# A fused attention and dense block on one core: how the feature weights are loaded and spread, and the order of the first steps

## The chip, the core and the metric

The kernel runs on one core of a Trainium2 chip, as one launch. The core has five engines with a queue each: TensorE (PE; its weight loads are listed apart, as PEld), VectorE (DVE), ScalarE (ACT), GpSimd (POOL) and SyncE (SP), which here issues most of the transfers. An engine works through its queue in order; a step that needs another engine's result waits on a semaphore, and all that is queued behind it on its own engine waits with it. The metric is the device time of one execution in microseconds, the median of several runs.

## The reference, cut to what matters

```python
xn = _layernorm(x)                                   # x: 2048 tokens x 512
qkv = xn @ wqkv                                      # 32 heads of 16
pq = einsum("bhsd,hdf->bhsf", q, w_phi)              # w_phi: 32 x 16 x 16
pk = einsum("bhsd,hdf->bhsf", k, w_phi)
phi_q = concatenate([softmax(pq), softmax(-pq)])     # over 16 features
phi_k = concatenate([softmax(pk), softmax(-pk)])
kv = einsum("bhsf,bhsd->bhfd", phi_k, v);  z = phi_k summed over tokens
o = einsum("bhqf,bhfd->bhqd", phi_q, kv) / (einsum("bhqf,bhf->bhq", phi_q, z) + 1e-6)
h = xn @ w1 + b1                                     # 1792 hidden
return x + o @ wo + (h * tanh(softplus(h))) @ w2     # Mish
```

All inputs are bf16. Since k is used only through `w_phi`, the kernel multiplies the keys' weights and `w_phi` into one matrix first: the logits of the keys' features are `xn @ (wk @ blockdiag(w_phi))`. It does the same for the queries later.

## The kernel before

The 2048 tokens are 16 tiles of 128, in four groups of four. The whole program is one list of short steps, `STEPS` (L24 to L59), each with a name and numbers; a table (`run`, L627) maps the name to a function. The order in the list is the order in which each engine gets its work, since the schedule is made by hand (`tc.manual_schedule()`, L129); nothing reorders it afterwards. `@n` is the PSUM bank of a product, and a last letter `a`, `v` or `p` the engine of a copy or an operation (ScalarE, VectorE, GpSimd). What stands ahead of the list in the code, L475 to L520, is queued first.

The steps of the head, as far as the change touches them:

- The loads ahead of the list: token tiles 0 and 1 (L478), the first half of the keys' weights as they lie (`wkp[:, 0:2]`, L482), the other half through a transposing transfer into `wT` (L483), tiles 2 and 3 (L489), the values' weights `wv` (L490), half of `w1` (L491), tokens 4 to 7 (L492), the other half of `w1` (L493), all from SyncE; the bias `b1` and `w_phi` from ScalarE (L486, L488). `w_phi` comes in its final layout `wsrc`: 128 partitions, with four pieces of 16 elements in each.
- The constants: `ident` for turning with TensorE, `block` (ones where a row and a column belong to the same head), both made on GpSimd, and warm-ups: 12 products of ones that nobody reads (L519), nine of 512 columns and three of 128, in bank 5.
- `LS i`, `RS i`, `AZ i`: a tile's statistics (VectorE), its inverse root (ScalarE with Ln and Exp, or GpSimd) and its centring (VectorE). `TP i` turns the tile by four products with `ident`, `TC i` copies it into `xnT`.
- `TW kt` turns a quarter of the keys' weights from `wkp`, `TK kt` copies it into `wT`. `KM` makes the masks. `WB` (L527) multiplies `block` with `wsrc` into `Wbd`, the block diagonal of `w_phi` in four pieces. `F0 kt` folds: four products of `wT` with `Wbd`; `FD kt` copies the folded quarter back into `wkp`.
- `LP` (L197): the key logits of tiles 0 and 1, eight products of 512 columns, alternating between the tiles. `L s i` are the logits of the other tiles, `LC` their copy, `V t` and `VC t` the values and their copy, `H u` and `M u` the hidden layer's product and its Mish (with the bias `b1f`, made by `PB`, `CB`). `E`, `X`, `S` are the features (differences to the extremes, exponentials, sums). `AM` loads ScalarE's table for Mish. `LN g` and `AP g k` are statistics and centring of a later group, turned by transposing transfers. `DX`, `DW` load later tokens and weights.

TensorE's queue before: warm-ups, `PB`, `TW 0`, `TW 1`, `TP 0`, `TP 1`, `F0 0` to `F0 3`, `LP`, `V 1`, `TP 2`, `V 0`, `TP 3`, `L 0 2`, `H 0`, `L 0 3`, `H 1` and so on.

Of the kernel before, what the change touches and what calls it, by code (L numbers as in the profile page):

```python
# [8 lines left out]
BF16 = mybir.dt.bfloat16  # L9
# [3 lines left out]
ALU = mybir.AluOpType  # L13
# [17 lines left out]
DW 2; E 0 1; X 0 1; LN 2; LC 1 0 v; LC 1 3 v; WL 1; LN 3; AP 2 0; AP 2 1; X 0 0; V 6 @3; M 10; M 11;  # L31
M 12; H 14 @5; S 0 0; WL 2; LC 1 2 a; VC 6 a; M 13; AP 3 0; H 15 @0; H 16 @2; H 17 @1; LC 1 1 a; AP
3 1; WT; H 18 @3; H 19 @4; M 14; M 15; M 16; M 17; H 20 @5; M 18; M 19; H 21 @0; H 22 @2; H 23 @1; H
24 @3; M 20; M 21; H 25 @4; H 26 @5; M 22; M 23; H 27 @0; M 24; M 25; M 26; M 27; H 28 @2; M 28; H
29 @1; M 29; E 1 0; E 1 1; S 0 1; L 2 1 @3; L 2 0 @4; LC 2 0 v; L 2 2 @5; LC 2 1 v; L 2 3 @0; F 0
@2; R 0 0 a; L 3 2 @1; R 0 1 a; LC 2 2 v; LC 2 3 a; FC 0 a; X 1 0; F 1 @4; F 2 @3; FC 2 a; N 0 0; L
3 0 @5; V 9 @0; LC 3 0 a; V 3 @2; VC 3 a; LC 3 2 v; A 0 0; VC 9 a; V 7 @1; F 3 @3; V 2 @5; VC 7 a; V
8 @2; L 3 3 @0; FC 3 a; X 1 1; VC 2 a; FC 1 v; E 2 0; L 4 0 @4; DW 3; LC 3 3 a; E 2 1; V 4 @1; N 0
1; VC 8 v; X 2 0; S 1 1; LC 4 0 a; S 1 0; L 4 3 @3; VC 4 a; L 4 2 @5; V 11 @0; A 0 1; LC 4 2 a; V 5
@2; VC 11 a; R 1 1 a; S 2 0; L 4 1 @4; LC 4 1 a; L 3 1 @1; VC 5 a; LC 3 1 a; H 30 @5; H 31 @0; LC 4  # L40
3 v; R 1 0 a; M 30; H 32 @4; M 31; M 32; H 33 @2; M 33; N 1 1; H 34 @1; H 35 @3; H 36 @5; M 34; H 37
@0; M 35; H 38 @4; E 3 0; H 39 @2; H 40 @1; M 36; N 1 0; M 37; M 38; M 39; H 41 @3; H 42 @5; H 43
@0; M 40; A 1 0; M 41; E 3 1; M 42; M 43; A 1 1; X 2 1; V 12 @4; VC 12 a; L 5 0 @2; V 10 @1; V 15
# [19 lines left out]
def kernel(  # L63
# [12 lines left out]
    nc = tc.nc  # L76
    P = 128
# [15 lines left out]
    wphi_v = A_w_phi.rearrange("(j i) a b -> (i a) j b", j=4)  # L93
# [18 lines left out]
    wsrc = wts.tile([P, 4, DH], BF16, name="wsrc")  # L112
    wv = wts.tile([P, KT, D], BF16, name="wv")
# [8 lines left out]
    ident = consts.tile([P, P], BF16, name="ident")  # L122
    mhalf = consts.tile([P, TPG], FP32, name="mhalf")
# [9 lines left out]
    tables = ["natural_log_exp_and_others"]  # L133
# [343 lines left out]
    for t in range(2):  # L477
        nc.sync.dma_start(x_sb[:, t, :], x_v[:, t, :])  # L478


    wT_of = {0: lnp.tile([P, 4, 512], BF16, name="wT", tag="xn")}
    nc.sync.dma_start(wkp[:, 0:2, :], wqkv_v[:, 0:2, D : 2 * D])  # L482
    nc.sync.dma_start_transpose(  # L483
        out=wT_of[0][:, :, 2 * P : 4 * P], in_=A_wqkv[2 * P : 4 * P, D : 2 * D]
    )
# [3 lines left out]
    nc.sync.dma_start(x_sb[:, 2:4, :], x_v[:, 2:4, :])  # L489
    nc.sync.dma_start(wv[:], wqkv_v[:, :, 2 * D : 3 * D])  # L490
    nc.sync.dma_start(w1_sb[:, :, 0 : 7 * P], w1_v[:, :, 0 : 7 * P])  # L491
    nc.sync.dma_start(x_sb[:, 4:8, :], x_v[:, 4:8, :])  # L492
    nc.sync.dma_start(w1_sb[:, :, 7 * P : F], w1_v[:, :, 7 * P : F])  # L493

    nc.scalar.preload_act_table_set(tables[0])
    make_identity(nc, ident[:])

    nc.gpsimd.memset(block[:], 1.0)
# [6 lines left out]
    nc.gpsimd.memset(mhalf[:], -0.5)  # L505
    nc.gpsimd.memset(eps[:], 1e-5)
# [12 lines left out]
    for n in (512,) * WARM + (P,) * SHORT:  # L519
        dummy(n)  # L520

# [5 lines left out]
    def weights_by_block():  # L527
        nc.vector.tensor_tensor(
            out=Wbd[:].rearrange("p j (h e) -> p j h e", h=8),
            in0=block[:, None, :, :].to_broadcast([P, 4, 8, 16]),  # L530
            in1=wsrc[:, :, None, :].to_broadcast([P, 4, 8, 16]),
            op=ALU.mult,
        )
# [89 lines left out]
    def load_queries():  # L623
# [4 lines left out]
        "KM": masks, "AW": lambda: dummy(P), "WB": weights_by_block, "PB": bias,  # L628
        "AM": lambda: table("mish"), "CB": lambda: nc.vector.tensor_copy(b1f[:], pf_of.pop("b")[:, 0:FT]),
        "LS": first_stats, "RS": first_root, "AZ": first_apply, "TP": first_turn,  # L630
        "TW": turn_keys, "TK": lambda kt, c: keep_keys(kt, copies[c]),
# [49 lines left out]
```

## Time and profile before

| | us |
|---|---|
| runs before | 173.4, 173.81, 174.56 |
| median | 173.81 |
| span of the profiled execution (first to last instruction) | 172.0 |
| TensorE busy within it | 168.0 |
| VectorE, ScalarE busy | 143.9, 123.8 |
| GpSimd busy | 7.8 |

The profile's own execution is told by its span; what lies between that and the device time (start and end of the program) is not in the trace. Times in the views are microseconds from the span's start. In a row of the timeline stand start, duration, engine, line, operation, what it writes and reads, and how often; in brackets the idle time of the engine before it and what ended that. The chain of waits follows the work back from the last instruction: at each step to what released it, or to the instruction before it on its engine. A transfer's time runs from its issue to its landing.

### The profile page before, as it was taken

What the parts mean: (1) busy time and instruction counts of PE and PEld (TensorE: products, weight loads), DVE (VectorE), ACT (ScalarE), POOL (GpSimd) and SP (SyncE); (2) the same over time, 40 slices, a digit from 0 to 9 for tenths busy, and PEclk for the clock granted to TensorE, in tenths of its full rate; (3) what the DMA queues carried; (4) which work ended last, traced back from release to release, by engine and by line L of the source; (5) the groups of instructions that cost most, each with busy time, mean ns of one, the idle gap of its engine ahead of it and who ended that gap; (6) DMA issues with size and microseconds to landing.
All of it is one profiled execution on the core that took longest, in us unless ns stands there. A gap on an engine that the chain in (4) does not pass through costs nothing.

```text
span 172.0 us, 2735 instructions
## 1 busy us (share of the span) xinstructions
PE 168.0 (98%) x1047; PEld 82.6 (48%) x1047; DVE 143.9 (84%) x223; ACT 123.8 (72%) x199; POOL 7.8 (5%) x23
## 2 busy tenths in 40 slices
PE   8899999999999999999999999999999999999993
PEld 2554444444454544454445644544444444554452
DVE  3869998999599999969989999799799998884333
ACT  2778899997999989889978989977282792432200
POOL 4123002300000000000000000000000000000000
PEclk9999999999999999999999999999999999999999
DMA  4997299589000000000000194309335618668941
GB/s 124 303 370 248 54 255 347 99 162 228 21 0 0 0 4 0 0 0 0 4 0 0 36 113 99 61 9 150 90 97 116 153 52 197 146 134 216 110 131 61
DMA packets 44185, 18.02 MB, mean 105 GB/s; under 512 B 35980, under 2 KB 44172, under 8 KB 44172
## 3 DMA queue, kind: packets, MB, share of 16 engines
q1 hardware_dynamic: 43472, 17.73, 43.9%
q8 instruction: 8, 0.13, 0.4%
q10 hardware_dynamic: 700, 0.12, 0.4%
q14 instruction: 5, 0.04, 0.1%
HBM read 7.10 MB, written 2.10 MB: 53 GB/s over the span
## 4 chain that ended last, share of the span: by engine, by line
PE 95%; DMA 2%; SPq 0%; ACT 0%; issue 0%; DVE 0%
PE po L457 28%; PE ph L223 28%; PE pl L189 14%; PE po L464 8%; PE pv L189 8%; PE pnd L412 2%; PE pkv L381 2%; DMA wkp<-in_A_wqkv_dram 2%; PE pl L204 1%; PE pfold L151 1%; PE pwide L189 1%; SPq L478 0%; PE ptr L569 0%; PE ptw L576 0%; ACT wT L582 0%
## 5 line engine op out<-in xcount | busy, mean ns | idle before, releaser
L457 PE MATMUL po<-w_sb,acts 128*128 128x512 bf16 (+2 forms) x238 | 50.8, 366 | 0.0
L223 PE MATMUL ph<-xnT,w_sb 128*128 128x512 bf16 x224 | 49.8, 379 | 0.0
L234 ACT ACTIVATE acts<-ph,b1f 128x512 bf16<-128x512 f32 x56 | 36.3, 701 | 4.2 <-PE ph L223 4.0
L300 DVE TENSOR_REDUCE s<-e 128x128 f32<-128x2048 bf16 x16 | 36.1, 2276 | 0.5 <-ACT e L283 0.5
L223 PEld LDWEIGHTS <-w_sb 128*128 128x128 bf16 x224 | 21.7, 98 | 25.7
L457 PEld LDWEIGHTS <-acts 128*128 128x128 bf16 x238 | 22.1, 98 | 23.6
L283 ACT ACTIVATE e<-e 128x2048 bf16<-128x2048 bf16 x16 | 30.5, 1919 | 0.0
L189 PEld LDWEIGHTS <-xnT 128*128 128x128 bf16 x184 | 17.5, 98 | 19.6
L471 DVE TENSOR_TENSOR x_sb<-po,x_sb 128x512 bf16<-128x512 f32 (+2 forms) x17 | 11.0, 656 | 8.4 <-PE po L464 8.4
L464 PE MATMUL po<-wqk,xnT 128*128 128x512 bf16 (+2 forms) x68 | 15.6, 366 | 0.0
L189 PE MATMUL pv<-wv,xnT 128*128 128x512 bf16 x64 | 15.6, 379 | 0.0
L189 PE MATMUL pl<-wqk,xnT 128*128 128x512 bf16 x64 | 15.4, 379 | 0.0
L427 ACT COPY ds<-pnd 128x32 f32<-128x32 f32 x16 | 2.9, 182 | 16.5 <-PE pnd L412 16.5
L247 ACT CAST p_sb<-pl 128x512 bf16<-128x512 f32 x21 | 12.2, 594 | 3.6 <-PE pl L189 3.4
L139 ACT ACT_TABLE_LOAD x10 | 12.8, 1283 | 0.2
L258 DVE TENSOR_TENSOR m<-m 128x512 bf16<-128x512 bf16 (+1 forms) x32 | 11.5, 359 | 1.1
L189 PE MATMUL pl<-wkp,xnT 128*128 128x512 bf16 x48 | 11.7, 379 | 0.0
L267 DVE TENSOR_TENSOR e<-p_sb,m 128x2048 bf16<-128x2048 bf16 x8 | 9.8, 1226 | 1.8 <-PE pkv L381 1.5
L258 DVE TENSOR_TENSOR m<-p_sb 128x1024 bf16<-128x1024 bf16 x16 | 10.9, 681 | 0.0
L165 DVE BATCH_NORM_STATS2 stats<-x_sb 128x6 f32<-128x512 bf16 x16 | 10.1, 677 | 0.9 <-DMA x_sb<-in_A_x_dram 0.9
L267 DVE TENSOR_TENSOR e<-m,p_sb 128x2048 bf16<-128x2048 bf16 x8 | 9.8, 1225 | 0.3
L334 DVE TENSOR_TENSOR e<-e,r 128x2048 bf16<-128x2048 bf16 x8 | 9.6, 1216 | 0.5 <-ACT r L309 0.5
(68 smaller groups left out, 133.9 us busy)
## 6 DMA issues: line engine op xcount, KB each, us to landing
w_sb<-in_B_w_dram SPq DMA_DIRECT2D x4, 896.0 KB, 7.8
out_dram<-x_sb SPq DMA_DIRECT2D x15, 128.0 KB, 1.8
x_sb<-in_A_x_dram SPq DMA_DIRECT2D x3, 512.0 KB, 7.5
wv<-in_A_wqkv_dram SPq DMA_DIRECT2D x1, 512.0 KB, 4.6
wqk<-in_A_wo_dram SPq DMA_DIRECT2D x1, 512.0 KB, 4.9
x_sb<-in_A_x_dram SPq DMA_DIRECT2D x2, 128.0 KB, 2.1
wkp<-in_A_wqkv_dram SPq DMA_DIRECT2D x1, 256.0 KB, 3.6
x_sb<-in_A_x_dram SPq DMA_DIRECT2D x1, 256.0 KB, 3.6
```

The costliest lines, as they stand in the source:

```text
L139: nc.scalar.preload_act_table_set(name)
L189: nc.tensor.matmul(pp, lhsT=xnT[:, t, kt, :], rhs=w[:, kt, :], start=(kt == 0), stop=(kt == KT - 1),)
L223: nc.tensor.matmul(ph_of[u][:], lhsT=w1_sb[:, kt, f * P : (f + 1) * P], rhs=xnT[:, g * TPG : (g + 1) * TPG, kt, :], start=(kt == 0), stop= ...
L234: nc.scalar.activation(acts[:, f, g * 512 : (g + 1) * 512], ph_of.pop(u)[:], ACT.Mish, bias=b1f[:, f : f + 1])
L247: copy(p_of[s][:, i, :], pl_of.pop((s, i)))
L258: nc.vector.tensor_tensor(out=m[:], in0=src[:, :, 0:half], in1=src[:, :, half : 2 * half], op=op)
L267: nc.vector.tensor_tensor(out=e_of[s][:].rearrange("p t j l c -> p (t j) l c")[:, :, pl, :].rearrange("p t (c e o) -> p t c e o", e=8, o=2 ...
L283: nc.scalar.activation(v, v, ACT.Exp)
L300: nc.vector.reduce_sum(t[:], pair(s, k).rearrange("p t j l (c e) -> p (t j l c) e", e=16), axis=AX.X)
L457: nc.tensor.matmul(po_of[t, c.stop][:, c], lhsT=acts[:, f, t * P : (t + 1) * P], rhs=w2_sb[:, f, c], start=(f == 0), stop=False,)
L464: nc.tensor.matmul(po_of[t, c.stop][:, c], lhsT=oT_of[t // 2][:, t % 2 * 4 + j, :], rhs=wo_sb[:, j, c], start=False, stop=(j == 3),)
L471: nc.vector.tensor_tensor(out=y, in0=po_of.pop((t, c.stop))[:, c], in1=y, op=ALU.add)
```

## The change

Five things change together.

1. `w_phi` is loaded by rows into a new tile `wraw` (128 partitions with one piece of 64 elements each), and a new step `WX` spreads it into the layout of `wsrc` by 16 small products with a selection matrix `sel`; `WC` copies the result from PSUM. `sel` lies in the space of `kvm`, which is used much later.
2. The warm-ups become steps: `AW 512` or `AW 128`. They stand before, around and behind `WX`: in all seven of 512 and two of 128 columns.
3. The loads become steps (`D`), and the half of the keys' weights goes ahead of token tile 1.
4. `WB` can run on GpSimd (`WB p`), and does. The clearing of constants goes from GpSimd to VectorE, and ScalarE's first table is loaded by the first step that needs it.
5. The steps of the head are in another order and partly on other engines, up to the hidden products of the first group. From `H 13` on the list is as it was.

```diff
-WARM, SHORT = 9, 3
 STEPS = """
-KM; LS 0; RS 0 p; LS 1; RS 1 a; DX 2; PB @0; AZ 0; AZ 1; TW 0 @1; TW 1 @2; TP 0 @3; TP 1 @4; TK 0 a;
-TK 1 a; WB; F0 0 @5; FD 0 a; F0 1 @1; TC 0 v; F0 2 @2; F0 3 @3; FD 2 a; TC 1 v; FD 1 v; FD 3 a; LP i
-@4,5; LS 2; LS 3; RS 2 a; LC 0 0 a; V 1 @1; RS 3 p; AZ 2; TP 2 @2; TC 2 a; VC 1 a; AM; V 0 @3; LC 0
-1 v; AZ 3; CB; TP 3 @4; TC 3 v; L 0 2 @5; LC 0 2 a; H 0 @0; M 0; L 0 3 @2; LC 0 3 a; H 1 @1; M 1; H
-2 @4; M 2; H 3 @5; H 4 @0; H 5 @2; VC 0 a; H 6 @1; M 3; M 4; M 5; H 7 @4; M 6; M 7; H 8 @3; H 9 @5;
-H 10 @0; M 8; H 11 @2; H 12 @1; LN 1; M 9; E 0 0; AP 1 0; AP 1 1; H 13 @4; L 1 0 @3; DX 3; L 1 3 @5;
+D x001 s; AW 512; AW 512; AW 512; AW 512; AW 512; AW 128; D phi a; D wn02 s; D b1 a; D x011 s; AW
+512; WX @3; AW 512; LS 0; D wt1 s; WC v; WB p; AW 128; TW 1 @5; KM; RS 0 a; TW 0 @3; TK 1 a; LS 1;
+F0 1 @2; TK 0 v; F0 0 @0; AZ 0; TP 0 @1; D x022 s; RS 1 a; FD 1 a; FD 0 a; AZ 1; PB @4; TC 0 v; TP 1
+@5; F0 2 @2; F0 3 @3; FD 2 a; TC 1 v; LS 2; D wv s; CB; RS 2 p; LS 3; FD 3 a; AZ 2; D w10007 s; LP i
+@0,1; RS 3 p; V 0 @2; AZ 3; TP 2 @5; V 1 @3; LC 0 0 a; TC 2 a; D x044 s; LC 0 1 v; TP 3 @5; TC 3 a;
+TL; L 0 2 @0; H 4 @5; M 4; D w10714 s; VC 0 v; L 0 3 @2; VC 1 v; DX 2; LC 0 2 v; H 6 @1; H 1 @5; LN
+1; H 2 @3; H 3 @0; LC 0 3 a; H 0 @2; M 2; M 6; M 1; H 5 @3; E 0 0; AM; M 3; H 9 @1; M 0; H 7 @4; M
+9; AP 1 0; H 8 @5; H 12 @1; H 11 @2; M 7; H 10 @0; AP 1 1; H 13 @4; M 5; L 1 0 @3; DX 3; M 8; L 1 3
...
-    wphi_v = A_w_phi.rearrange("(j i) a b -> (i a) j b", j=4)
+    wraw = wts.tile([P, 4 * DH], BF16, name="wraw")
+    sel = kvm[:].rearrange("p k c -> p (k c)")[:, 0 : 4 * P + 4]
-    tables = ["natural_log_exp_and_others"]
+    tables = [""]
...
-    nc.scalar.dma_start(b1b[:], b1_v[:, :])
-    with nc.allow_non_contiguous_dma(reason="tiny w_phi load"):
-        nc.scalar.dma_start(wsrc[:], wphi_v)
...
+    def load(what, on):
+        q = {"s": nc.sync, "a": nc.scalar}[on]
...
+        elif what == "phi":
+            q.dma_start(wraw[:], A_w_phi.rearrange("h (c a) b -> (h c) (a b)", c=4))
...
+    nc.vector.memset(ident[:], 0.0)
+    nc.vector.memset(block[:], 1.0)
+    nc.vector.memset(sel, 0.0)
+    nc.vector.memset(eps[:], 1e-5)
+    nc.vector.memset(mhalf[:], -0.5)
+    nc.gpsimd.affine_select(
+        out=ident[:], in_=ident[:], pattern=[[-1, P]], compare_op=ALU.not_equal,
+        fill=1.0, base=0, channel_multiplier=1,
     )
...
+    nc.gpsimd.affine_select(
+        out=sel, in_=sel, pattern=[[1, 4 * P + 4]], compare_op=ALU.not_equal,
+        fill=1.0, base=-3, channel_multiplier=-4,
+    )
...
-    for n in (512,) * WARM + (P,) * SHORT:
-        dummy(n)
...
+    def spread(b):
+        pf_of["x"] = bank(b, "pspread")
+        for j in range(4):
+            for a in range(4):
+                nc.tensor.matmul(
+                    pf_of["x"][:, j * DH : (j + 1) * DH],
+                    lhsT=sel[:, j * P + 3 - a : (j + 1) * P + 3 - a],
+                    rhs=wraw[:, a * DH : (a + 1) * DH],
+                    start=(j == 0 and a == 0), stop=(a == 3), skip_group_check=True,
+                )
 
-    def weights_by_block():
-        nc.vector.tensor_tensor(
+    def weights_by_block(on):
+        {"v": nc.vector, "p": nc.gpsimd}[on].tensor_tensor(
...
         if on == "a":
+            table("natural_log_exp_and_others")
             nc.scalar.activation(r, mv[:, i, 1:2], ACT.Ln, bias=eps[:])
...
+        "WC": lambda c: copies[c](wsrc[:].rearrange("p j b -> p (j b)"), pf_of.pop("x")[:, 0 : 4 * DH]),
```

On SyncE's queue the order becomes: tile 0, keys' half, tile 1, transposed half, tiles 2 and 3, `wv`, and on as before; on ScalarE's: `w_phi`, then `b1`. TensorE's queue becomes: warm-ups and `WX`, `TW 1`, `TW 0`, `F0 1`, `F0 0`, `TP 0`, `PB`, `TP 1`, `F0 2`, `F0 3`, `LP`, `V 0`, `TP 2`, `V 1`, `TP 3`, `L 0 2`, `H 4`, `L 0 3`, `H 6`, `H 1`, `H 2`, `H 3`, `H 0`, `H 5`, `H 9`, `H 7`, `H 8`, `H 12`, `H 11`, `H 10`, `H 13`. VectorE's: the five clearings, `LS 0`, `WC`, `KM`, `LS 1`, `TK 0`, `AZ 0`, `AZ 1`, `TC 0`, `TC 1`, `LS 2`, `CB`, `LS 3`, `AZ 2`, `AZ 3`, `LC 0 1`, `VC 0`, `VC 1`, `LC 0 2`, `LN 1`. ScalarE's: both loads, a table, `RS 0`, `TK 1`, `RS 1`, `FD 1`, `FD 0`, `FD 2`, `FD 3`, `LC 0 0`, `TC 2`, `TC 3`, the table for Mish, `M 4`.

More of the change, by code (lines that the diff above doesn't have):

```diff
@@ L6 @@
 from concourse._compat import with_exitstack
-from concourse.masks import make_identity
 BF16 = mybir.dt.bfloat16
@@ L35 @@
[L35 to L43, printed above, removed]
+D x001 s; AW 512; AW 512; AW 512; AW 512; AW 512; AW 128; D phi a; D wn02 s; D b1 a; D x011 s; AW
@@ L504 @@
         )
-    nc.gpsimd.memset(mhalf[:], -0.5)
-    nc.gpsimd.memset(eps[:], 1e-5)
     for i in range(2):
@@ L627 @@
     run = {
-        "KM": masks, "AW": lambda: dummy(P), "WB": weights_by_block, "PB": bias,
+        "KM": masks, "AW": dummy, "WB": weights_by_block, "PB": bias, "WX": spread,
+        "WC": lambda c: copies[c](wsrc[:].rearrange("p j b -> p (j b)"), pf_of.pop("x")[:, 0 : 4 * DH]),
         "AM": lambda: table("mish"), "CB": lambda: nc.vector.tensor_copy(b1f[:], pf_of.pop("b")[:, 0:FT]),
@@ L631 @@
         "TW": turn_keys, "TK": lambda kt, c: keep_keys(kt, copies[c]),
+        "D": load, "TL": lambda: table("natural_log_exp_and_others"),
         "LP": first_logits, "TC": lambda i, c: first_keep(i, copies[c]),
```

46 lines of the change are left out of this document (29 added, 17 removed).

## The prediction

> **What bounds the kernel now.** I read the page first, then the whole chain of waits, then its first 16 us, then the timeline of those microseconds. From the page:
>
> ```profile
> span 172.0 us, 2735 instructions
> PE 168.0 (98%) x1047; PEld 82.6 (48%) x1047; DVE 143.9 (84%) x223; ACT 123.8 (72%) x199; POOL 7.8 (5%) x23
> ...
> PE 95%; DMA 2%; SPq 0%; ACT 0%; issue 0%; DVE 0%
> ...
> L234 ACT ACTIVATE acts<-ph,b1f 128x512 bf16<-128x512 f32 x56 | 36.3, 701 | 4.2 <-PE ph L223 4.0
> ```
>
> TensorE carries 95% of the chain, so the end moves only with TensorE's work, with holes in it, or with the moment at which its unbroken stream begins. A piece of the whole chain (start, length, what) and the chain's first stretch:
>
> ```profile
> 74.94 1.02 PE pkv L381 x32
> ```
>
> ```profile
> 1.24 0.43 SPq L478
> 1.67 0.05 issue
> 1.72 3.59 DMA wkp<-in_A_wqkv_dram
> 5.31 0.05 issue
> 5.36 0.62 PE ptw L576 x8
> 5.98 0.24 PE ptr L569 x4
> 6.22 0.06 issue
> 6.28 0.60 ACT wT L582
> 6.88 0.05 issue
> 6.92 0.84 PE pfold L151 x12
> 7.77 1.79 PE pl L204 x8
> 9.56 0.86 PE pv L189 x4
> ```
>
> The stream starts when half of the keys' weights lands at 5.31; after one short wait for ScalarE it is unbroken from 7.77, and the first logits (LP) end at 9.56. I use that 9.56 as the mark: everything behind it is TensorE's work, which the change leaves as it is. Prices: a product of 512 columns 0.86 / 4 = 0.215, one of 128 columns 0.24 / 4 = 0.06, one of 65 columns 1.02 / 32 = 0.032, a hand-over 0.05 to 0.06.
>
> The span is 172.0 and the median of the runs 173.81, so 1.8 us lie around it. I work in the span and add 1.8.
>
> **What the head costs, by rows of its timeline.**
>
> ```profile
> 0.83 4.00 PE L514 MATMUL warm<-const-bfloat16-1.0 128*128 128x512 bf16 x12 [0.83 <-PEq L665]
> ...
> 1.58 0.75 POOL L500 TENSOR_SCALAR_AFFINE_SELECT block<-block 128x128 bf16<-128x128 bf16 x2
> ...
> 2.37 0.22 DVE L523 TENSOR_TENSOR KVmask<-block 128x64 f32<-128x64 bf16 x1 [2.37 <-POOL block L500]
> ...
> 2.95 0.69 DVE L165 BATCH_NORM_STATS2 stats<-x_sb 128x6 f32<-128x512 bf16 x1 [0.35 <-DMA x_sb<-in_A_x_dram]
> 3.34 0.15 PEld L514 LDWEIGHTS <-const-bfloat16-1.0 128*128 128x128 bf16 x1 [0.28 <-issue]
> ...
> 3.77 0.15 PEld L514 LDWEIGHTS <-const-bfloat16-1.0 128*128 128x128 bf16 x1 [0.28 <-issue]
> 3.77 0.66 DVE L165 BATCH_NORM_STATS2 stats<-x_sb 128x6 f32<-128x512 bf16 x1
> ...
> 4.17 0.46 SPq L490 DMA_DIRECT2D wv<-in_A_wqkv_dram  x1
> ...
> 4.87 0.85 DVE L176 TENSOR_SCALAR xn<-x_sb,mv,rstd 128x512 bf16<-128x512 bf16 x2 [0.22 <-POOL rstd L172]
> ...
> 5.64 0.42 DVE L528 TENSOR_TENSOR Wbd<-block,wsrc 128x512 bf16<-128x512 bf16 x1
> ...
> 5.79 1.07 ACT L582 CAST wT<-ptw 128x512 bf16<-128x512 f32 x2 [0.51 <-PE ptw L576]
> ...
> 6.24 0.76 DVE L588 COPY xnT<-ptr 128x512 bf16<-128x512 bf16 x2 [0.18 <-PE ptr L569]
> ...
> 7.36 0.69 DVE L160 CAST wkp<-pfold 128x512 bf16<-128x512 f32 x1 [0.36 <-PE pfold L151]
> ...
> 7.97 0.68 DVE L165 BATCH_NORM_STATS2 stats<-x_sb 128x6 f32<-128x512 bf16 x1
> ...
> 11.07 0.17 DVE L629 CAST b1f<-pb 128x14 f32<-128x14 bf16 x1
> ```
>
> Start to start, a tile's statistics take VectorE 3.77 - 2.95 = 0.82 and a 512-wide copy out of PSUM 7.97 - 7.36 = 0.61; centring a tile takes 0.39. The four products of a turn end their issue at 5.36 + 0.24 = 5.60 and their copy starts at 5.79: 0.19 from TensorE to a reader. A warm-up product of 512 takes 3.77 - 3.34 = 0.43, twice the 0.215 of later: TensorE runs at half pace here.
>
> **The change, part by part.** *The selection matmuls (WX).* TensorE's queue becomes five warm-ups of 512, one of 128, one of 512, then 16 products of 16 columns: 0.83 + 5 x 0.43 + 0.11 + 0.43 = 3.52. No row has products of 16 columns. Below, they cost next to nothing (16 columns are a quarter of 65); above, twice 0.032, at half pace: 1.02 in all. I take 16 x 0.032 = 0.51, since 16 columns at half pace stream less than 65 at full pace do. WX is through at 4.03. Its selection matrix is one more select on GpSimd, 516 wide: with 0.375 for 128 (0.75 for two), up to 1.5 us, which ends it near 3 from a start like the 1.58 of today. The feature weights now come as 128 pieces of 128 bytes, not 512 of 32, first in ScalarE's queue.
>
> ```profile
> wv<-in_A_wqkv_dram SPq DMA_DIRECT2D x1, 512.0 KB, 4.6
> ...
> x_sb<-in_A_x_dram SPq DMA_DIRECT2D x2, 128.0 KB, 2.1
> ...
> wsrc<-in_A_w_phi_dram ACTq DMA_DIRECT2D x1, 16.0 KB, 4.0
> ```
>
> At best they take the 2.1 of a plain copy, at worst the 4.0 of today, from an issue near 0.8: 2.9 to 4.8. I take 2.9, as the copy in 128 pieces is the like one, so WX does not wait; at 4.8 it would cost 1.3. The bias now follows it there; its turn stands behind the first token turn and is wanted only by the first Mish, past 12 us.
>
> *Keys' half ahead of the second tile.* The half leaves 0.48 earlier (1.24, not 1.72) and no longer behind 128 KB. This gains nothing by itself, because the longest path now runs elsewhere. What is moved back is tile 1: it stands third on the queue, with the same 512 KB up to its end as the half had, which landed at 5.31; if 128 KB cost only the 0.45 between two issues, it lands near 4.3. I take 4.6, nearer to the lower end, for most of the small pieces that ran beside the half are gone.
>
> *VectorE's new queue.* It now holds the copy of the spread weights (WC), the masks (KM), tile 1's statistics, a key copy (TK 0, ScalarE's before), both centrings, both token copies. WC waits for TensorE, and all of these stand behind it. WC starts at 4.03 + 0.19 = 4.22 and takes 0.22 (between 0.17 for 14 columns and 0.69 for 512); KM 0.22; statistics from 4.66, key copy from 5.48, centring from 6.09 and 6.48, done at 6.89. Turning tile 1 then takes TensorE from 6.95 to 7.19; the two last folds are through at 7.67, before the token copy (7.19 + 0.19, then 0.38: 7.76). The second of the logits' eight products needs that copy: it starts at 7.82 and the eighth ends at 7.82 + 7 x 0.215 = 9.33. The mark is 9.56: **0.23 earlier**. The wait behind it is late next: ScalarE's four copies of the folded weights, 0.54 each (1.07 for two), the last two behind the last folds from 7.6 to 8.75, just ahead of the seventh product at 8.9. The gained stretch could not be much longer anyway: the values need a load that was issued at 4.17 and landed 4.6 later, at 8.8.
>
> *The block product (WB) on GpSimd.* VectorE is rid of 0.42. The bound below is that 0.42; above, GpSimd's 0.375 for 128 elements of one input, times four, times two inputs: 3.0. I take four times 0.375 = 1.5: from 4.50 to 6.00. The folds wait for it at 6.05, and the second fold needs the key copy of 6.17 anyhow, so it is hidden up to about 1.6 and costs the rest in full beyond. [...]
>
> *Head's order anew.* The hidden products come in another order and two value copies and a logits copy (0.7 each) go from ScalarE to VectorE. TensorE's list of products up to the second group's logits is of the same length. VectorE's extra 2.1, less a token copy, must fit here:
>
> ```profile
> 12.76 2.47 DVE L165 BATCH_NORM_STATS2 stats<-x_sb 128x6 f32<-128x512 bf16 x4 [0.57 <-DMA x_sb<-in_A_x_dram]
> ...
> 19.13 2.63 SPq L181 DMA_TRANSPOSE xnT<-xn  x2
> ...
> 25.38 1.89 PE L189 MATMUL pl<-wkp,xnT 128*128 128x512 bf16 x8
> ```
>
> The statistics waited 0.57 for tokens, and the turned tokens are wanted only at 25.38, over 3 us after their transfers were issued by 21.76. A delay of about 1.1 stays hidden; without that cover it would cost 1.1. Of the banks, each hidden product finds its own free, as the Mish that empties it (0.70 against 0.86 for a unit's four products) is done at least a unit ahead. I cost this at nothing. The dropped and added memsets lie in time that VectorE idled until 2.37.
>
> **Rivals.**
> 1. *GpSimd's product is slow* and takes tile 1's place as the last wait. For it: it runs on the slowest engine, and two folds and both turns stand behind it on TensorE. Against: nothing but the scaling. It decides from 1.6 on; at 3.0 it ends at 7.50, the folds and turns (4 x 0.24) at 8.52, token copy at 9.09, logits at 9.15 + 1.51 = 10.66: 1.1 later than the mark, **174.9**.
> 2. *Tile 1 lands late.* At 5.31 statistics start at 5.36, 0.70 later than above: 10.03, **174.3**.
> 3. *TensorE stays at half pace.* The last quoted warm-up weight loads are 0.43 apart and the products of 5.36 run 0.06 apart, so the pace doubles after 2.9 to 4.5 us of nearly unbroken work (3.77 and 5.36, less 0.83). Now 16 tiny products stand in that stretch, and holes follow behind it (until 6.05 and 6.95). If they do not count as work, another such spell runs at half pace: some 3.5 us of stream, the middle of that span, lose half, 1.7, so 9.33 + 1.7: **175.3**. [...]
> 4. *WX is shorter than I think.* With almost no cost, 9.33 - 0.5 = 8.8, just when the values land: **173.0**.
> 5. *Nothing moves:* the gain of 0.23 is lost in another hand-over: **173.8**.
>
> **How the numbers follow.** Forecast: 172.0 - 0.23 + 1.8 = **173.6**, chance 0.50; rival 1 0.14, 2 0.12, 3 0.11, 4 0.08, 5 0.05. The three runs of before spread from 173.4 to 174.56, so 1% (1.7 us) is about what a measurement can tell from no change. The forecast's own range is 173.1 to 174.2: with WX at its upper bound, 0.51 later, it is 174.1. From rival 4, less a little, to rival 1: 172.7 to 174.9 holds eight in ten. Slower by over 1% (175.55) needs rival 3 at full price, or two of 1 to 3 together: 0.11. Faster by over 1% (172.07) would need more than the values' load allows: 0.04. Within: 0.85.
>
> **What would show it.** Right: WX's products end near 4.0 and the copy of the spread weights starts at 4.2; VectorE runs without a hole from there to 6.9; TensorE waits for VectorE's centring before the second turn; the first values begin near 9.3 and the chain is TensorE's from there. Wrong: folds released by GpSimd (rival 1), statistics of tile 1 released by its load (2), 0.43 between products after 5 us (3), or any TensorE hole from 12 to 30 us in the reordered hidden products.

## The result, and the profile after

| | before | after |
|---|---|---|
| median of the runs (us) | 173.89 (20 runs, 173.36 to 174.68) | 174.37 (20 runs, 173.78 to 175.89) |
| the profiled execution: time, span | span 172.0 | 175.6, span 173.9 |
| first logits end (the mark) | 9.56 | 11.51 |
| from there to the end of the span | 162.4 | 162.4 |

The ratio is 1.004, with a 95% interval of 1.0024 to 1.0057: no faster, and a little slower, where 0.23 us less was forecast. All of it happens ahead of the mark; behind it the span is as long as before.

The 20 times are not spread evenly: 13 lie in 173.78 to 174.46, none between that and 175.09, and 7 in 175.09 to 175.89. The profiled execution, 175.6, is one of these upper ones, above 175.0. Ten more times of the same kernel, taken with the experiments, gave five in 173.9 to 174.16, one of 174.79 and four near 175.4. So there are two things to explain: what all 30 have in common (the lower 19 have a median of 174.06), and what befalls 11 of the 30. The kernel before has no such group: none of its 20 executions lies above 175.0, nor any of the 100 that were taken beside the experiments.

The page of the kernel after; of its last row each digit is a fortieth of the span, in tenths of full speed:

```profile
span 173.9 us, 2763 instructions
PE 169.1 (97%) x1060; PEld 83.9 (48%) x1060; DVE 145.8 (84%) x230; ACT 122.4 (70%) x197; POOL 9.1 (5%) x21
...
PEclk9789999999999999999999999999999999999999
```

TensorE is still the bound. Its clock, 9 throughout in the kernel before, shows a 7 and an 8 in the second and third slice. The chain of waits of its head (start, length, what):

```profile
1.71 3.37 DMA x_sb<-in_A_x_dram
...
5.10 0.70 DVE stats L166
...
6.01 0.59 DVE wT L606
...
6.64 0.40 PE pfold L152 x4
7.04 0.53 PE ptr L593 x4
7.57 0.12 PE pb L560
7.70 0.54 PE ptr L593 x4
8.23 0.85 PE pfold L152 x8
9.09 2.42 PE pl L205 x8
11.51 0.86 PE pv L190 x4
```

It begins with the second token tile now, not with the keys' half, and that tile lands at 5.08, not at 4.6. From there to 6.64 the path is VectorE's; then it is TensorE's without a hole. But its rows are longer than the prices of before: the four products of a turn take 0.53, where they took 0.24, and eight logits products 2.42, where they took 1.79. Two stretches of equal length show why (length, busy time of TensorE, weight loads, VectorE, ScalarE and GpSimd with their instructions, then the granted clock, the busy share of the transfers and GB/s):

```profile
3.55:6.97 3.42, 2.09 (x36) 1.50 (x34) 2.56 (x9) 1.97 (x6) 1.15 (x1) 1.00 0.95 225
6.97:10.39 3.42, 3.42 (x23) 2.30 (x22) 2.73 (x8) 1.74 (x4) 0.70 (x2) 0.50 1.04 376
```

From 6.97 to 10.39 the clock is at 0.50, after a stretch of the same 3.42 us in which TensorE was busy for 2.09. In finer slices the clock falls at 6.95 and is back at 10.36, 3.41 us later. At half pace 3.42 us lose 1.71.

The record has the mean granted clock of each execution too. One such spell in 173.9 us leaves 1 - 1.71/173.9 = 0.990, and of the 11 upper executions two have 0.99, this one and that of 175.89. The other nine have 1.00. That doesn't mean that they kept their pace: a profile without a clock row counts as 1.00 (five of the 16 profiles here have none), and so does a pace that doubles late, as `e2_tile1_act` will show. The fall is thus seen in two of the eleven; what the other nine went through isn't on record.

The rows of the timeline that answer to the prediction's steps:

```profile
3.44 0.59 PE L543 MATMUL pspread<-wraw,kvm 128*128 128x16 bf16 x16
...
4.07 0.23 DVE L653 CAST wsrc<-pspread 128x64 bf16<-128x64 f32 x1
...
4.45 1.15 POOL L551 TENSOR_TENSOR Wbd<-block,wsrc 128x512 bf16<-128x512 bf16 x1 [1.47 <-DVE KVmask L534]
...
5.10 0.69 DVE L166 BATCH_NORM_STATS2 stats<-x_sb 128x6 f32<-128x512 bf16 x1 [0.68 <-DMA x_sb<-in_A_x_dram]
...
5.66 0.38 PE L152 MATMUL pfold<-Wbd,wT 128*128 128x128 bf16 x4 [0.67 <-POOL Wbd L551]
...
6.64 0.40 PE L152 MATMUL pfold<-Wbd,wT 128*128 128x128 bf16 x4 [0.61 <-DVE wT L606]
```

The selection products are where they were forecast. VectorE stood idle for 0.68 until the tile came, and TensorE's two long holes, 0.67 and 0.61, end with GpSimd's block product and with VectorE's key copy.

### The profile page after: what moved, and what is told of

Read it like the earlier page. It is cut to its first block, busy times and chain, and to the rows that moved or that the text cites. A ratio compares the mean times of both kernels' runs of the same rounds, so it can differ in the third digit from the quotient of the medians.

```text
span 173.9 us, 2763 instructions
## 1 busy us (share of the span) xinstructions
PE 169.1 (97%) x1060; PEld 83.9 (48%) x1060; DVE 145.8 (84%) x230; ACT 122.4 (70%) x197; POOL 9.1 (5%) x21
## 4 chain that ended last, share of the span: by engine, by line
PE 95%; DMA 2%; DVE 1%; SPq 0%; issue 0%
PE po L458 28%; PE ph L224 28%; PE pl L190 14%; PE po L465 8%; PE pv L190 8%; PE pnd L413 2%; PE pkv L382 2%; DMA x_sb<-in_A_x_dram 2%; PE pl L205 1%; PE pfold L152 1%; PE pwide L190 1%; PE ptr L593 1%; DVE stats L166 0%; DVE wT L606 0%; SPq L490 0%; SPq L485 0%
## 5 line engine op out<-in xcount | busy, mean ns | idle before, releaser
L235 ACT ACTIVATE acts<-ph,b1f 128x512 bf16<-128x512 f32 x56 | 35.6, 704 | 5.3 <-PE ph L224 5.1
L248 ACT CAST p_sb<-pl 128x512 bf16<-128x512 f32 x20 | 11.6, 595 | 5.0 <-PE pl L190 3.4
```

The lines of the kernel that those rows point to most:

```text
L235: nc.scalar.activation(acts[:, f, g * 512 : (g + 1) * 512], ph_of.pop(u)[:], ACT.Mish, bias=b1f[:, f : f + 1])
L248: copy(p_of[s][:, i, :], pl_of.pop((s, i)))
```

## The experiments

The theory ahead of the experiments had two parts. One: tile 1's late landing costs all executions some tenths. Two: in a part of them TensorE falls back to half pace in the head, because too little work stands there. The rivals were that the selection products themselves do it, that the small pieces of the feature weights hold up the other loads, and that the loss comes from later in the kernel.

### Filling the holes, and the tile from the other queue

`e1_fill` puts warm-ups into two holes, `e2_tile1_act` issues tile 1 from ScalarE's queue, `e3_both` does both. Where warm-ups stand in the holes (`e1_fill`, `e3_both` and `e6_tiny_late`), all warm-ups write bank 4 and not bank 5, which the turns use. The ratios of this section are to executions of the kernel before that were taken together with the variant (medians 173.66 to 173.85).

```diff
-... RS 0 a; TW 0 @3; TK 1 a; LS 1; F0 1 @2; TK 0 v; ...
+... RS 0 a; TW 0 @3; AW 512; AW 512; AW 512; TK 1 a; LS 1; F0 1 @2; AW 512; AW 512; AW 512; TK 0 v; ...
-... D wn02 s; D b1 a; D x011 s; ...
+... D wn02 s; D x011 a; D b1 a; ...
```

> Two sets of three warm-ups of 512 in TensorE's holes, ahead of the first and of the second fold. Theory A (the holes between 4.9 and 6.9 let TensorE fall to half pace for a spell of 3.4 us in some executions, and tile 1's late landing costs the rest): the group of executions above 175 goes, the others stay near 174.1, so the median is 174.0 to 174.3. Rival B (the slow group has another cause, such as late transfers): a third of the executions stays above 175, median 174.3 to 174.6. Rival C (the fill itself delays the folds): all executions 0.2 to 0.5 later.

> Tile 1 is loaded from ScalarE's queue, right behind the feature weights; the keys' half keeps its place. Theory A: tile 1 lands by about 4.2, its statistics start at about 4.45, not 5.10, the logits end 0.6 earlier, the lower group lies at 173.4 to 173.7, and the holes are shorter, so that fewer executions fall to half pace. Rival D (tile 1 is not what VectorE's queue waits for; the key copy or GpSimd's product is): the lower group stays near 174.0.

> Both edits at once. Theory A: one group only, 173.3 to 173.7, the fastest of these kernels, 0.2 to 0.5 below the kernel before. Rival B: still a group 1.2 to 1.7 above the other. Rival D: one group near 174.0.

Measured: `e1_fill` 175.24 (174.57 to 175.6), ratio 1.0078 [1.0056, 1.01]; `e2_tile1_act` 174.19, eight of twelve in 173.83 to 174.45 and four in 175.29 to 175.47, ratio 1.0043 [1.0019, 1.0066]; `e3_both` 175.18 (174.96 to 175.71), ratio 1.0084 [1.0064, 1.0103]. None of the three gained what the theory gave it: `e1_fill` has four of six above 175.0, the lower eight of `e2_tile1_act` have a median of 173.96, where 173.4 to 173.7 was expected, and `e3_both` is among the slowest.

In the profile of `e1_fill` (174.57) TensorE runs at full pace (three of the fillers take 0.65 from 6.08 on) and its logits end at 9.83, 1.7 earlier than in the kernel after: the half pace is worth what the clock row says. The time does not follow, though. Its chain of waits near the end of the kernel:

```profile
152.79 0.94 PE po L465 x5
153.73 4.47 DMA qT<-e
...
158.25 0.43 PE pnd L413 x8
```

TensorE waits there for a transposing transfer that nobody waited for before. I come back to it below. That profile is the fastest of its six executions; why the other five are up to 1 us slower was not seen.

Of `e2_tile1_act` the profile (175.29) is one of the upper executions. The tile's statistics start at 4.72, but now the keys' half is late:

```profile
1.23 3.69 DMA wkp<-in_A_wqkv_dram
...
4.97 0.62 PE ptw L600 x4
```

Four turning products take 0.62 there, where the chain of `e7_tile1_first`, further below, has 0.41. Half pace lasts until about 9.4 us: from 4.97 to 9.1 its products of 128 columns start 0.107 apart, twice the 0.056 of full pace. Yet its clock row shows 1.00 all the time. Half pace from the start isn't shown by that row (nor is it in the warm-ups, whose products are 0.43 apart with 1.00 beside them). Only a fall is shown. So an upper execution can come about in two ways: the pace falls back, or it doubles late. And TensorE counts 3.08 us busy between 2.58 and 6.00 in this execution, which did not double its pace by then. In `e3_both` (profile 175.19, full pace) the logits end at 10.22, since the six fillers themselves stand on the path, and TensorE waits 0.7 for the late transfer.

### The feature weights loaded straight into place

`e4_direct` goes back to loading `w_phi` in 512 pieces into `wsrc`; one warm-up takes the place of the selection products.

```diff
-... AW 512; WX @3; AW 512; LS 0; D wt1 s; WC v; WB p; ...
+... AW 512; AW 512; AW 512; LS 0; D wt1 s; WB p; ...
```

> The changed kernel with the feature weights loaded in 512 pieces as before; the selection matmuls and their copy are out, one warm-up of 512 stands in their place. If the small pieces slow the other transfers: tile 1 and the keys' half land 0.3 or more later than 5.08 and 4.04, and the lower group lies 0.2 to 0.5 above 174.1. If they do not: the landings stay, VectorE is 0.2 shorter, but the block product starts when the pieces land, at 4.8 instead of 4.45, and the time is within 0.2 of the changed kernel.

Measured: 174.24 (173.85 to 174.59, 11 runs), none above 175.0; ratio 1.0026 [1.0011, 1.004]. The chain of its head:

```profile
1.71 3.14 DMA x_sb<-in_A_x_dram
...
4.87 0.71 DVE stats L167
...
5.78 0.59 DVE wT L608
...
6.41 0.40 PE pfold L153 x4
6.81 0.32 PE ptr L595 x4
7.13 0.11 PE pb L562
7.24 0.33 PE ptr L595 x4
7.57 0.45 PE pfold L153 x8
8.02 1.76 PE pl L206 x8
9.77 0.86 PE pv L191 x4
```

This is the head at full pace. GpSimd's block product starts at 3.22 here, 1.2 earlier than in the kernel after (4.45), and the chain is the same: neither it nor the selection products set the end. The tile lands at 4.85 with the small pieces beside it, so they don't hold it up. The upper executions are gone.

### Narrow products of ones in their place; the order of two loads; more narrow ones before

`e5_tiny` is `e4_direct` with sixteen warm-ups of 16 columns where the selection products stood; `e6_tiny_late` has them in a hole behind `TW 0` instead; `e7_tile1_first` is the kernel after with tile 1 ahead of the keys' half again; `e8_before_tiny` is the kernel before with sixteen narrow warm-ups among its own.

```diff
 e5_tiny:        -AW 512; AW 512; AW 512; LS 0;    +AW 512; AW 16 (16 times); AW 512; LS 0;
 e6_tiny_late:   -TW 0 @3; TK 1 a;                 +TW 0 @3; AW 16 (16 times); TK 1 a;
 e7_tile1_first: -D wn02 s; D b1 a; D x011 s;      +D x011 s; D wn02 s; D b1 a;
 e8_before_tiny: -for n in (512,) * WARM + (P,) * SHORT:
                 +for n in (512,) * 6 + (16,) * 16 + (512,) * 2 + (P,) * SHORT:
```

> The kernel with the direct load of the feature weights, but 16 warm-ups of 16 columns stand where the one of 512 stood; their results go nowhere, nothing waits for them. TensorE's queue is as long as in the changed kernel. Theory A (tiny products count for little in the stretch that doubles TensorE's pace, and the holes behind them keep it low): a third of the executions lies 1.2 to 1.7 above the others, as in the changed kernel; lower group 173.9 to 174.5. Theory C (holes alone make the group, and the direct load had none by chance): also a group, in this run and the next. Theory E (the feature weights' products themselves, through their waits): no group.

> The same 16 tiny warm-ups, but in the first hole behind the keys' turning products; the warm-up ahead is dense again. Queue as long as in the changed kernel. Theory A: no upper group, 173.8 to 174.6 like the direct load. Theory B (it is the length of TensorE's queue, which shifts its instruction loads against other transfers): an upper group in this run as in the one before.

> The changed kernel with the loads in the old order: tile 1 ahead of the keys' half. Tile 1 lands near 3.4, the half near 5.0. Theory A with the late tile as the rest of the loss: the statistics of tile 1 start at 4.4, not 5.1; the key copy waits for the turned keys until about 5.7, not 5.93; the lower group comes 0.2 to 0.3 down, to 173.8 to 173.9; the upper group stays, 1.2 to 1.7 above, and is no smaller, as TensorE's first hole (4.3 to 5.0) now lies before the keys' products. Rival: the load order is worth the full 0.6 (173.5).

> The kernel before, with 16 warm-ups of 16 columns in place of three of 512 behind the first six, two of 512 and three of 128 behind. Its stream has no holes behind 5.4. The warm-up is about 0.8 shorter. Theory A (tiny products and holes together): some executions double their pace late, but the dense stream from 5.4 bounds the loss; median 173.7 to 174.6, spread wider than 1.2. Theory of tiny products alone: an upper group of a third, 1.2 to 1.7 above the rest. Theory of holes alone: 173.8 as before.

| | median | above 175.0 | ratio |
|---|---|---|---|
| `e5_tiny` | 174.13 | 1 of 12 | 1.0025 [1.0006, 1.0045] |
| `e6_tiny_late` | 174.24 | 0 of 12 | 1.0027 [1.0012, 1.0042] |
| `e7_tile1_first` | 174.20 | 4 of 12 | 1.0038 [1.0015, 1.006] |
| `e8_before_tiny` | 174.30 | 0 of 12 | 1.0019 [1.0002, 1.0037] |

Putting tile 1 first again gains nothing. The chain of `e7_tile1_first` (profile 174.29, full pace) begins with the other load:

```profile
1.71 3.20 DMA wkp<-in_A_wqkv_dram
...
4.95 0.41 PE ptw L600 x4
...
7.97 1.76 PE pl L205 x8
9.72 0.86 PE pv L190 x4
```

In these kernels, whichever of the two stands third lands at 4.85 to 5.1, and the logits end at 9.7 to 9.8 either way. In the profiles of `e5_tiny` and `e6_tiny_late` something else was late: the values' weights took 5.9 us from issue to landing, where 4.6 was the row of before, and the values began at 10.17 and 10.14.

### The kernel after once more

> The changed kernel itself, once more, for a second profile and for more times. The theory: its executions fall into two groups, near 174.1 and near 175.4, and the upper ones are those in which TensorE falls to half pace for some 3.4 us from about 7 us on. By it a third of the executions lie in 175.0 to 175.9 and the rest in 173.8 to 174.5. If the profiled execution is one of the lower ones, its products of 512 columns run about 0.22 apart from 7 us on, the first logits end at 9.7 to 9.8 and the span is about 172.3; if it is one of the upper ones, it again shows products 0.43 apart and logits that end at 11 or later. The rival: the upper group comes from something late in the kernel, and then an upper profile ends its first logits before 10, or a lower one shows the half pace too.

Measured: 174.48, 173.9 to 175.42 in ten runs, four of them above 175.0; ratio 1.005 [1.0026, 1.0073]. The profiled execution (174.79) is not an upper one. Its profile has no clock row, so that the 1.00 in the line below tells nothing by itself; but behind 4.7 its products run at full pace (the last eight of the folds start 0.056 apart), so the pace did not fall. Its stretch of the same length, and the end of its head:

```profile
3.55:6.97 3.42, 2.63 (x39) 1.73 (x37) 2.87 (x9) 2.19 (x7) 1.15 (x1) 1.00 0.95 218
```

```profile
4.22 6.25 DMA wv<-in_A_wqkv_dram
...
10.52 1.04 PE pv L190 x4
```

The products of 512 columns end near 9.76, as in `e4_direct`. Then TensorE waits 0.8 for the values' weights, whose load took 6.25 in this execution and 5.0 in the first profile of the same kernel. So one kernel's two profiles show the two heads: with the fall of the clock 11.51, without it 9.76, 1.75 apart.

### Which part does it: order alone, work alone, products alone

`e10_half_first` is the kernel before with the keys' half ahead of tile 1 and nothing else; `e12_half_act` is the kernel before with that half on ScalarE's queue. `e11_hole` is `e4_direct` without the warm-up that had taken the selection products' place. `e13_wx_more` is the kernel after with one more warm-up behind the selection products. `e14_wx_unread` loads the feature weights straight into place and still runs the selection products, on the same operands, for nobody; so it loads the feature weights twice.

```diff
 e10_half_first: -for t in range(2): nc.sync.dma_start(x_sb[:, t, :], ...)
                 -nc.sync.dma_start(wkp[:, 0:2, :], ...)
                 +nc.sync.dma_start(x_sb[:, 0, :], ...)
                 +nc.sync.dma_start(wkp[:, 0:2, :], ...)
                 +nc.sync.dma_start(x_sb[:, 1, :], ...)
 e12_half_act:   -nc.sync.dma_start(wkp[:, 0:2, :], ...)
                 +nc.scalar.dma_start(wkp[:, 0:2, :], ...)     (ahead of b1)
 e11_hole:       -AW 512; AW 512; AW 512; LS 0;               +AW 512; AW 512; LS 0;
 e13_wx_more:    -AW 512; WX @3; AW 512; LS 0;                +AW 512; WX @3; AW 512; AW 512; LS 0;
 e14_wx_unread:  -AW 512; AW 512; AW 512; LS 0; (e4_direct)   +AW 512; WX @3; AW 512; LS 0;
```

> The kernel before, with one part of the change alone: the natural half of the keys' weights is issued ahead of the second tile. The theory: whichever transfer stands third on the queue lands at 4.9 to 5.1, so this only swaps which of the two is late; the half lands near 4.1, the turn of the keys' weights starts near 4.9 (the warm-ups end at 4.83), the second tile lands near 5.0 and its centring ends near 6.5, its turn near 6.8 and its copy near 7.4; the first logits end between 9.3 and 9.7, that is within 0.25 of the 9.56 of before, and the time is within 0.3 of before. A rival: the order was what the change gained by, and without the other parts the logits end at 9.0 or earlier, 0.5 faster. Another: the late second tile costs its full delay, as in the changed kernel, logits at 9.9 or later, 0.3 slower or more.

> The changed kernel with the feature weights loaded straight into place (no selection products, no copy of them), and with nothing on TensorE where the selection products were: its warm-ups are then the changed kernel's own, seven of 512 columns and two of 128, without the tiny products among them. It computes the same. The question is whether the spells of half pace come from too little work on TensorE before and between the turns, or from the tiny products themselves. If from too little work, at least 2 of the 12 executions lie above 175.0. If from the tiny products, none does, and the times are those of the variant with one more warm-up of 512 columns, 173.8 to 174.6, median near 174.2.

> The kernel before, with the natural half of the keys' weights issued from ScalarE's queue, ahead of the bias and the feature weights there, so that neither it nor the second tile stands behind the other. The theory (the moment at which the three first transfers have all landed is set by how much they move together, not by their order): the half lands between 4.2 and 4.9 instead of 5.31, the feature weights some 0.45 later than before (near 5.9), the turn of the keys' weights starts at 4.85 to 4.95, and the first logits end 0.2 to 0.5 earlier than 9.56; the time is 0 to 0.4 below that of before (ratio 0.998 to 1.000), less than that where the values' weights, which land at 8.8, become the wait. A rival: the feature weights, now issued later, hold the block product and the folds, and the logits end as before or later (ratio 1.000 to 1.003).

> The changed kernel with one more warm-up of 512 columns behind the selection products, so that the full-width work of TensorE ahead of the turns is that of the variant with directly loaded weights and eight such warm-ups (0 of 11 executions above 175.0). If the spells come from work that is missing, at most 1 of 12 executions lies above 175.0 and the median is 174.0 to 174.3. If they come from the selection products themselves, about a third still does (3 to 6 of 12). The first logits of a profile at full pace end at 9.7 to 9.9 either way, since the turns of the keys' weights are not what is late.

> The changed kernel with the feature weights loaded straight into place, while the selection products run where they ran, on the same operands (the weights are loaded by rows too), and nobody reads their result. It computes the same. Sixteen products of ones, as narrow, in their place gave 1 of 12 executions above 175.0. If the selection products' own operands bring the spells, about a third of the executions lies above 175.0 (3 to 6 of 12) though nothing waits for the products. If it was the chain that hangs on them (copy of the result, block product on GpSimd, first fold), at most 1 of 12 does, and the rest lie at 173.9 to 174.5.

| | median | above 175.0 | ratio |
|---|---|---|---|
| `e10_half_first` | 174.62 | 1 of 8 | 1.0064 [1.0039, 1.0088] |
| `e11_hole` | 174.14 | 2 of 12 | 1.004 [1.0017, 1.0063] |
| `e12_half_act` | 174.93 | 3 of 6 | 1.0086 [1.0057, 1.0115] |
| `e13_wx_more` | 174.21 | 0 of 12 | 1.0031 [1.0019, 1.0043] |
| `e14_wx_unread` | 175.69 | 5 of 6 | 1.0109 [1.0084, 1.0134] |

`e10_half_first`: I had expected a swap without a price; it costs 0.9 (173.72 for the kernel before, taken together with it). The half landed at about 4.05, 1.3 earlier than before, but tile 1 at 5.45 in the profile:

```profile
1.70 3.75 DMA x_sb<-in_A_x_dram
...
5.47 0.71 DVE stats L165
```

In the kernel before these statistics started at 3.77. On VectorE they stand ahead of both centrings, so the turn of tile 0 waits as well: its centring starts at 6.30, not at 4.87. Of the change, then, this part alone makes the kernel slower, and the rest of the new list takes most of it back. That it does so by the key copies and folds ahead of the turns is read from the list; no run tried it. `e12_half_act` missed too: on the other queue the half also delays tile 1, whose place on its own queue was not touched: it landed 3.50 after its issue, at 4.75, where the kernel before has 2.0; and the bias behind it holds TensorE's small bias product, ahead of the turns, until 5.07. What these loads shared here was more than a queue.

`e13_wx_more` keeps the selection products, the holes behind them, GpSimd's product and the order of the loads, adds 0.43 us of work, and has no upper execution left in 12, where the kernel after had 11 of 30 (at that rate, 12 without one would come up about 4 times in 1000: (19/30)^12). `e14_wx_unread`, taken on the same chip beside it, has five of six, so it isn't the chip. `e11_hole` has no selection products and 0.43 less of work than `e4_direct`, and has 2 of 12, which is too few to set it apart from the 0 of 11 there. `e10_half_first` has neither narrow products nor anything else of the change, and in the one execution above 175.0, which is the profiled one, its clock falls too. `e14_wx_unread`, where the keys' half happened to land at 4.95 in the profile (issue 1.25 and 3.7) and tile 1 at 5.27, and where nothing waits for the selection products, has 5 of 6; of these five, two have a mean clock of 0.99 and two 0.999, which leaves no room for a fall. The stretches of 3.42 us before and of the fall, of `e10_half_first` and then of `e14_wx_unread`:

```profile
4.25:7.67 3.42, 1.75 (x21) 1.16 (x20) 1.80 (x5) 1.16 (x4) 0.47 (x1) 1.00 1.11 258
7.67:11.09 3.42, 3.42 (x24) 2.36 (x23) 2.86 (x7) 2.46 (x6) 0.00 (x0) 0.50 1.06 364
```

```profile
4.25:7.67 3.42, 2.12 (x25) 1.30 (x24) 2.17 (x6) 2.26 (x7) 1.15 (x1) 1.00 1.00 248
7.67:11.09 3.42, 3.20 (x17) 2.05 (x19) 2.80 (x8) 1.26 (x3) 1.39 (x4) 0.50 1.04 380
```

The table has each profile's emptiest stretch of 3.42 us that starts between 3.4 and 5.2. Beside it stands how often the kernel lay above 175.0. Where the profile has no clock row (`e4_direct`, `e5_tiny`, `e7_tile1_first`, `e8_before_tiny` and the second of the kernel after), that the clock did not fall is read from the distance of the products:

| | least busy in 3.42 us | clock fell in the profile | above 175.0 |
|---|---|---|---|
| `e10_half_first` | 1.74 | yes | 1 of 8 |
| after (first profile) | 2.09 | yes | 11 of 30 |
| `e14_wx_unread` | 2.12 | yes | 5 of 6 |
| `e12_half_act` | 2.26 | no | 3 of 6 |
| `e7_tile1_first` | 2.45 | no | 4 of 12 |
| `e4_direct`, `e5_tiny` | 2.50, 2.54 | no | 0 of 11, 1 of 12 |
| after (second profile) | 2.63 | no | as above |
| `e11_hole` | 2.74 | no | 2 of 12 |
| before, `e13_wx_more` | 2.90, 2.91 | no | 0 of 120, 0 of 12 |
| `e8_before_tiny`, `e6_tiny_late` | 3.09, 3.12 | no | 0 of 12, 0 of 12 |

All profiles with 2.12 or less show the fall, none with 2.26 or more does, and no kernel whose profile kept 2.90 or more has an execution above 175.0. (`e1_fill` and `e3_both`, full as they are, are left out, as their times are moved by the fillers and by the late transfer; `e2_tile1_act` has 2.82 and shows the other form, a pace that doubles late.) The column is a hint, not a threshold: products at half pace count twice the time (0.43 against 0.215 for 512 columns), and the turns of the keys' weights, 219 ns each at full pace, took 311 in the profile of `e11_hole`, from 4.3 to 5.0, and up to 308 in that of `e13_wx_more`, from 5.1 on. What removes the upper group is shown by the executions of `e13_wx_more`, not by its 2.91. Nor do few busy microseconds in one profile foretell how often the group comes: `e10_half_first`, the emptiest, has it once in eight.

## Why the prediction was wrong, point by point

- **What bounds the kernel, and the mark.** Right. What lies behind the first logits has the same length before and after, 162.4 us, so the new order of the hidden products and the copies moved to VectorE cost nothing, as costed.
- **The selection products.** Taken at 0.51 from 3.52 on; they came 27 ns apart, from 3.44 to 3.87, with the copy at 4.07 instead of 4.22. The feature weights landed 2.5 after their issue, at about 3.3, where 2.1 and 2.9 were taken. Right, and a little better than taken, but not on the path: rival 4 would have turned that into a gain, and it did not. That the 128 pieces are what makes the load short was not borne out: issued first on ScalarE's queue, the 512 pieces of `e4_direct` took 2.3, against the 4.0 of before, where the bias stood ahead of them.
- **The block product on GpSimd.** 1.15, where 1.5 was taken from a select's 0.375 for 128 elements; VectorE had taken 0.42 for the same product in the kernel before. It ended at 5.60 and held the first folds by some tenths. `e4_direct`, where it starts at 3.22, has the same chain, so rival 1 fell.
- **Tile 1's landing, the step that failed in all executions.** "I take 4.6, nearer to the lower end, for most of the small pieces that ran beside the half are gone." It was 5.08 and about 4.84 in the two profiles; and the reason given was wrong as well, since with the small pieces back (`e4_direct`) it was 4.85. The nearer row was the one that the sum had as its upper bound, the third place on the queue in the kernel before, 5.31. Rival 2 is thus the direction it took, at a smaller size: 4.85 alone adds about 0.2 to the forecast's 9.33. `e10_half_first` shows that a late tile 1 costs time; that it is what the kernel after pays is read from the chain, since no run brought it earlier without making another load late.
- **The rest of the chain.** From the statistics to the key copy, through two turns with the bias product between them (0.32 + 0.11 + 0.33, where a turn was priced at 0.24), the sum was another 0.2 short. Together the logits end at 9.77, not at 9.33: 0.21 later than before instead of 0.23 earlier. This is about what the lower 19 of the 30 executions show, with a median of 174.06 against 173.89; where the values' weights come late as well (6.25 in the second profile), 0.8 is added. That load was taken to land at 8.8 from one row of before, and its 4.6 was 4.5 in the profile of `e11_hole` and 6.25 in the second of the kernel after.
- **TensorE's pace, the step that failed in a third of them.** Rival 3 was priced well, 1.7 (measured 1.75 between the two profiles), and given 0.11; a group that is later by about that much came in 11 of 30. The sum took for granted that the pace doubles with the warm-ups and then stays. The first profile shows it fall; for nine of the eleven the record doesn't say whether it fell or doubled late. What `e13_wx_more` shows is that 0.43 us more of work behind the selection products removes the group (0 of 12 above 175.0, against 11 of 30): work is missing there. That narrow products alone do it was not borne out: `e10_half_first` falls without any, `e8_before_tiny` keeps its pace with sixteen of them. The falls lasted 3.41 us in all three profiles that show one (6.95 to 10.36 here, 7.67 to 11.08 in `e10_half_first`, 7.67 to 11.09 in `e14_wx_unread`); the some 3.5 of rival 3 was an estimate from the moment at which the pace doubles in the kernel before, whose profile shows no fall. Why one kernel gives both heads, no run shows. TensorE's longest hole in the stretch before the fall was 0.67 here and 1.29 in `e10_half_first`.
- **Median and range.** The median moved by +0.48 where -0.23 was forecast; 174.37 lies outside the forecast's own range of 173.1 to 174.2, and within 172.7 to 174.9 only because the upper group, priced at 175.3, stayed a minority.
- **The signs.** Three of the signs of being wrong came together in the first profile: the first fold was released by GpSimd, tile 1's statistics by their load, and products stood 0.43 apart behind 5 us. By the chain, only the last two cost time.

What stays open: why the selection products with their own operands bring upper executions more often (5 of 6, 11 of 30) than as many narrow products of ones (1 of 12) with hardly more work beside them; in `e14_wx_unread` the keys' half was late too. Which of the two forms the other nine upper executions had, and how much work is enough for the pace to double and to stay, are open as well: the 3.08 us of `e2_tile1_act` were not enough. Why the values' weights took 4.5 us in one profile and 6.25 in another was not examined. No variant beat the kernel before.

## What to carry to other kernels

Moving one load ahead on a queue moved another one back (in `e10_half_first` the half from 5.31 to 4.05, tile 1 to 5.45), and what counts is who stands behind the one that is late: ask for the row of the place on the queue, not for the size of the transfer (third on the queue, the half of 256 KB landed at 4.91 in `e7_tile1_first` and tile 1 of 128 KB at 4.85 in `e4_direct`). Where an engine's pace goes with how busy it has been, as TensorE's did here, look for the emptiest stretch behind its warm-ups, of the length of a fall (3.4 us here), before taking a price at full pace: the profiles with 2.1 us or less of work in it fell back, those with 2.26 or more did not, and one warm-up of 0.43 us removed the upper group. When a kernel's times fall into two groups, one profile shows only one of them; take another of the same kernel before explaining the median, and read the pace from the distance of the products, as the clock row can be absent (in five of the 16 profiles here) or silent (1.00 throughout in `e2_tile1_act`, at half pace until about 9.4).

## What the runs showed of the hardware that was not expected

Four profiles (`e1_fill`, `e3_both`, `e7_tile1_first`, `e8_before_tiny`) show TensorE waiting near the end of the kernel, by 0.3 to 0.7 us, for a transposing transfer that is hidden in the others. The chain of `e8_before_tiny`, and the same place in the kernel before:

```profile
152.37 0.92 PE po L464 x5
153.29 4.54 DMA qT<-e
...
157.88 0.43 PE pnd L412 x8
```

```profile
154.51 3.02 PE po L457 x14
157.53 0.26 PE pnd L412 x8
```

The view of transfers between 154 and 158, of `e8_before_tiny` (queues with packets, megabytes and share, then the transfer with its median time from issue to landing), has an instruction load of queue 8 beside the transposes:

```profile
q8 instruction: 1, 0.02, 2.2%
...
qT<-e SPq DMA_TRANSPOSE x2, 4.4
```

In the kernel before there is none there, and the transfers take 2.8:

```profile
q14 instruction: 1, 0.01, 0.6%
...
qT<-e SPq DMA_TRANSPOSE x2, 2.8
```

Every page has eight such loads of queue 8, in the kernel before some 20 us apart. The last one falls at 155.5 to 156.0 in `e8_before_tiny` and before 158 in `e1_fill`, where TensorE waits, and at 158.0 to 162.0 in nine profiles without the wait, those of the kernel before and of the kernel after among them. In `e8_before_tiny` the view shows some 10 GB/s for over 1 us behind it, against 200 and more. That the load holds up the transposes fits these two, whose transposes took 4.4 and 4.0. In `e3_both` TensorE waits 0.7 for the same transfer, in `e7_tile1_first` 0.3 for a later one (`xnT<-wv`). No run moved the load alone, and what sets its moment was not shown. The load may be why `e8_before_tiny`, whose logits end at 9.40, is some 0.4 slower than the kernel before in the median.
